# Squaring a gate on ScalarE instead of GpSimd, in a recurrence with routed experts

## The chip, the cores and the metric

The kernel runs on one core of one Trainium2 chip. A core has five engines with an in-order queue each: TensorE (PE, its weight loads shown as PEld), VectorE (DVE), ScalarE (ACT), GpSimd (POOL) and SyncE (SP, which only issues DMAs here). POOL also issues DMAs: those whose rows are addressed by a list of indices. The metric is device time in microseconds; lower is better. The kernel before takes 990.24 us, the median of three runs (990.15 to 991.3).

## The reference

A gated linear recurrence over 4 sequences of 3648 steps and 256 channels, and behind it a mixture of 16 experts (4 groups of 4) to which each of the 14592 tokens is routed:

```python
log_a = c * sig_r * np.log(np.clip(a_base, 1e-06, 1.0 - 1e-06))
a_t = np.exp(log_a)
norm = np.sqrt(np.maximum(1.0 - a_t * a_t, 1e-06))
x_gated = norm * sig_i * x
for t in range(S):
    h = a_t[:, t] * h + x_gated[:, t]
    y[:, t] = h
# for each token: best group g, best expert e in it, weights from two softmaxes
h = np.maximum(xg[mask_e] @ w1[g, e], 0.0)          # 256 -> 1024
ye = h @ w2[g, e]                                   # 1024 -> 256
out[tok_idx] = combined[:, None] * ye
```

The `a_t * a_t` in `norm` is the square that this document is about.

## The kernel before

**Chunks.** Tokens lie along the free dimension, channels on the partitions in two halves. They are worked on in 16 chunks of `SIZES` tiles of 128 tokens (4, then thirteen times 8, then 4 and 2), so a full chunk is two tiles of 128 x 1024. For each half h of a chunk: `tanh_r` (ACT, L317) and `decay` (ACT Exp, L322) make the decay `a` in place; `square` (POOL, L327) writes a*a into a new tile `v`; `norm1` (DVE, L332) subtracts and clips; `norm2` (ACT Sqrt, L337) takes the root; `gate_i` (ACT, L341) and `gated` (DVE, L345) make the gated input; `scale_s` (DVE, L349) multiplies it into `v`; `scan` (DVE, L358) runs the recurrence and leaves the outputs in `a`.

**Routing.** PE turns the chunk's outputs into rows of tokens, with the routing logits beside them (`rows1`, L367, four fp32 matmuls for two tiles of 128 tokens; the profile counts eight, as each takes two passes). ACT copies the rows out of PSUM (`rows2`, L373), DVE sums the logits (`rows3`, L381). `route1` to `route3` (DVE L390 to L442, ACT Exp L397) pick the expert, `rank` (PE, L447 and L448) numbers the tokens of each expert, `route4` (DVE, L453 to L464) makes the row index `pi`, and `scatter` (POOL, L468) sends each tile of 128 rows with one indirect DMA into the experts' lists `y_s` in DRAM. The tiles for rows get token numbers from POOL (`rows0`, L378).

**Experts.** After chunks 2 and 3 four resident experts get a first block of 128 rows each (L1024 transposes on PE, L1028 copy on ACT, L1035 and L1047 matmuls, L1040 ReLU on ACT, L1052 and L1055 the result). After chunks 4, 7 and 10 counts are taken (L596, then a chain of small DVE operations L586 to L634, L643 on PE, L650 to L671), and from them comes a list of units of 256 rows of one expert. SP gathers a unit's rows (L478) and loads its weights (L974). Twelve units run in plain fp32 (`native`: L980 transposes, L990 and L1004 matmuls), the rest as three products of split operands (L859, L928). Results are weighted (L943 on ACT, L945 on DVE) and sent to the output by an indirect DMA of POOL (L951).

**Order.** Every operation is declared with `op(engine, cost, emit, due, after, new, use, ...)`. `Plan.run` simulates the engines with these costs and due times while the program is built and emits each operation when its turn comes; each engine then runs its own queue in that order, and semaphores keep the dependences. So a cost in an `op` doesn't change what an instruction does, but where it and others stand. An ACT operation can name a table (`exp`, `sqrt`); the planner charges a switch.

Of the kernel before, what the change touches and what calls it, by code (L numbers as in the profile page):

```python
# [12 lines left out]
AF = mybir.ActivationFunctionType  # L13
ALU = mybir.AluOpType
# [30 lines left out]
class Plan:  # L45
# [14 lines left out]
    def op(self, engine, cost, emit, due, after=(), new=(), use=(), dma=0, table=None, soon=0.0, order=()):  # L60
        o = Op(engine, cost, emit, due, new, use, dma, table, soon)
        after = dict.fromkeys(a for a in after if a)
        order = dict.fromkeys(a for a in order if a and a not in after)
        o.wait = len(after) + len(order)
        for b in o.new + o.use:
            b.left += 1
        for a in after:
            a.then.append(o)
        for a in order:
            a.next.append(o)  # L70
        self.ops.append(o)
        return o
# [70 lines left out]
def rglru_moe_kernel(ctx: ExitStack, tc: tile.TileContext, x, r_gate, i_gate, a_param,  # L143
                     w_group, w_expert, w1, w2, out):
    nc = tc.nc
    V, S, G, T, DMA = nc.vector, nc.scalar, nc.gpsimd, nc.tensor, nc.sync
# [33 lines left out]
    OTURN, ONORM1, ONORM2, OGATE, OGATED, OSCAN, OH, OROWS, OY = 5, 1, 14, 12, 13, 7, 4, 16, 20  # L180
    OROUTE, ORANK, OSCAT = (34, 34, 60), 46, 50
# [43 lines left out]
    op = plan.op  # L225
# [98 lines left out]
    def square(ck, h):  # L324
        ck.t["v", h] = pools["v"].tile([P, CH * P], F32, name="v")
        a = ck.t["a", h][:, :ck.W]
        G.tensor_tensor(ck.t["v", h][:, :ck.W], a, a, op=ALU.mult)  # L327


    def norm1(ck, h):  # L330
# [135 lines left out]
    def scatter(ck, ks):  # L466
        for k in ks:
            ins = G.indirect_dma_start(out=y_s, out_offset=bass.IndirectOffsetOnAxis(ap=ck.pi[:, k:k + 1], axis=0),  # L468
                                       in_=ck.t["yo", k // 4][:, k % 4, :], in_offset=None,
                                       bounds_check=NBLK * TS - 1, oob_is_err=False)  # L470
            tc.declare_no_dep(ins.ins, group="lst", reason="rows of one list are disjoint")
            tc.declare_no_dep(ins.ins, group="got", reason="what was read lies before the rows that still come")
            tc.add_to_no_dep_group("lst", ins.ins)
            tc.add_to_no_dep_group(f"lst{ck.c}", ins.ins)
# [28 lines left out]
    def act(n):  # L503
        return 0.16 + n / 1180
# [4 lines left out]
    def add_chunk(ck, before):  # L509
        K, W, due, b = ck.K, ck.W, ck.due, ck.b  # L510
        ld = {}
        for what in "asx":
            for h in range(2):
                if ck.c:
                    at = due + LOADS[what] + 3 * h
# [5 lines left out]
        sq = {}  # L521
        for h in range(2):
            th = op("ACT", act(W), lambda h=h: tanh_r(ck, h), due + h * OTURN, [ld["a", h]], use=[b["a", h]], table="exp")
            de = op("ACT", act(W) + 0.18, lambda h=h: decay(ck, h), due + h * OTURN, [th], use=[b["a", h]], table="exp")
            sq[h] = op("POOL", 0.05 + W * 1.95 / 1024, lambda h=h: square(ck, h), due + h * OTURN, [de], [b["v", h]], [b["a", h]])
        n1 = [op("DVE", 0.3 + W / 1920, lambda h=h: norm1(ck, h), due + ONORM1 + h * 4, [sq[h]], use=[b["v", h]]) for h in range(2)]
        n2 = op("ACT", 2 * act(W), lambda: norm2(ck), due + ONORM2, n1, use=[b["v", 0], b["v", 1]], table="sqrt")
        ga = []
# [29 lines left out]
        def at(o):  # L558
            return due + (ROUTE if early else o) + urgent
# [5 lines left out]
        rk = op("PE", 0.15, lambda: rank(ck), at(ORANK), [r3, before and before.acc], [q], [b["oe"]], order=[before and before.hold])  # L565
        r4a, r4 = chain(route4(ck), [0.33, 0.28, 0.28, 0.38, 0.17], at(ORANK), [rk], [b["pi"]], [b["oe"], q])
        ck.acc = r4a
        ck.sca = [op("POOL", 2.3, lambda k=k: scatter(ck, range(k, k + 2)), at(OSCAT), [r4],
                     use=[b["pi"], yos[k // 4]], dma=2 * P * DW * 4) for k in range(0, K, 2)]


# [681 lines left out]
    due = cks[-1].due  # L1253
# [90 lines left out]
```

## Time and profile before

| | before |
|---|---|
| median of 3 runs | 990.24 us |
| profiled execution | 991.88 us |
| its span, first to last instruction | 990.2 us |
| busy PE / PEld / DVE / ACT / POOL | 870.6 / 831.4 / 665.3 / 558.4 / 349.8 us |
| squares on POOL (L327), 32 in all | 56.6 us, mean 1784 ns |
| scatters (L468), 114 in all | 141.2 us, mean 1239 ns |
| mean granted TensorE clock | 0.954 |

The page divides the span into 40 slices of 24.8 us and gives each engine's busy share in tenths:

```profile
PE   1333578999998999999999999999999999999994
DVE  4987688945976742566777777777765576566661
ACT  7866566526875632355555565555654555454541
POOL 4264657827477466211111111111112122213122
PEclk9866599989999999999999999999999999999998
```

PE is thinly used in the first five slices and nearly full from the seventh on. A group of instructions is shown as busy time, mean of one, and the idle time of its engine just before them with what ended it. Times of one execution are in microseconds from the span's start; means of one instruction are in nanoseconds.

### The profile page before, as it was taken

To read this page: it belongs to the slowest core of one execution; us is meant where nothing else is said; L and a number is where in the kernel's file an instruction comes from. 1 tells how busy PE (TensorE), PEld (TensorE's weight loads), DVE (VectorE), ACT (ScalarE), POOL (GpSimd) and SP (SyncE) were. 2 spreads that over 40 slices of the span, in tenths; PEclk is the share of its full clock that TensorE was granted. 3 is DMA by queue.
4 is the path that set the end of the run, shared out by engine and by line. 5 is a ranking of instruction groups with operands and counts; after the bars stand their busy time and mean duration, and the time that the engine had idled before them with its cause. 6 is when DMAs were issued, how large, how long until landed. Compare 5 with 4: busy or idle time off the path is not lost. (4 is left out here: it accounts for less than half of the span.)

```text
span 990.2 us, 18521 instructions
## 1 busy us (share of the span) xinstructions
PE 870.6 (88%) x6082; PEld 831.4 (84%) x6082; DVE 665.3 (67%) x1366; ACT 558.4 (56%) x847; POOL 349.8 (35%) x322
## 2 busy tenths in 40 slices
PE   1333578999998999999999999999999999999994
PEld 1332568888887898899999999999999999999984
DVE  4987688945976742566777777777765576566661
ACT  7866566526875632355555565555654555454541
POOL 4264657827477466211111111111112122213122
PEclk9866599989999999999999999999999999999998
DMA  9995465696877857656766776678665465635310
GB/s 317 415 331 199 150 219 163 199 395 245 332 250 238 310 182 232 195 168 230 229 210 222 225 221 214 219 222 278 221 208 185 137 215 158 195 116 190 110 54 21
DMA packets 72455, 213.33 MB, mean 215 GB/s; under 512 B 10503, under 2 KB 28431, under 8 KB 68240
## 3 DMA queue, kind: packets, MB, share of 16 engines
q1 hardware_dynamic: 60464, 181.82, 55.6%
q0 software_dynamic: 11872, 30.05, 8.0%
q8 instruction: 59, 0.97, 0.4%
q14 instruction: 60, 0.49, 0.2%
HBM read 181.56 MB, written 32.36 MB: 216 GB/s over the span
## 5 line engine op out<-in xcount | busy, mean ns | idle before, releaser
L951 POOL DMA_INDIRECT out_dram<-o,cl x122 | 132.5, 1086 | 477.3 <-ACT o L943 265.7
L468 POOL DMA_INDIRECT y_s<-wf,pi x114 | 141.2, 1239 | 106.9 <-issue 51.2
L367 PE MATMUL q_y<-yw,a 128*128 128x148 f32 x368 | 66.5, 329 | 65.0 <-DVE a L358 39.5
L859 PE MATMUL q_h<-x,w1h 128*128 128x384 f32 (+1 forms) x512 | 116.6, 316 | 6.0 <-DVE i L866 5.3
L367 PEld LDWEIGHTS q_y<-yw,a 128*128 128x128 f32 x368 | 60.1, 219 | 72.7 <-DVE a L358 19.5
L866 DVE SCALAR_TENSOR_TENSOR i<-q_h,a 128x384 fp32r<-128x384 f32 (+1 forms) x128 | 61.8, 496 | 86.5 <-ACT a L863 84.5
L863 ACT ACTIVATE a<-q_h 128x384 fp32r<-128x384 f32 (+1 forms) x128 | 56.5, 447 | 109.3 <-PE q_h L859 93.1
L859 PE MATMUL q_h<-xh,w1h 128*128 128x256 f32 x400 | 113.6, 284 | 0.0
L859 PE MATMUL q_h<-xh,w1l 128*128 128x256 f32 x400 | 113.2, 283 | 0.0
L859 PE MATMUL q_h<-xl,w1h 128*128 128x256 f32 x400 | 113.2, 283 | 0.0
L863 ACT ACTIVATE hh<-q_h 128x512 fp32r<-128x512 f32 x100 | 60.2, 602 | 92.7 <-PE q_h L859 82.2
L814 DVE TENSOR_TENSOR w1l<-wf,w1h 128x1024 fp32r<-128x1024 f32 x82 | 99.9, 1221 | 11.8 <-ACT w1h L812 9.8
L866 DVE SCALAR_TENSOR_TENSOR hl<-q_h,hh 128x512 fp32r<-128x512 f32 x100 | 68.8, 688 | 55.8 <-ACT hh L863 55.7
L814 DVE TENSOR_TENSOR w2l<-wf,w2h 128x1024 fp32r<-128x1024 f32 x82 | 98.2, 1218 | 0.0
L859 PEld LDWEIGHTS q_h<-x,w1h 128*128 128x128 f32 x512 | 84.9, 190 | 7.6 <-issue 5.0
L812 ACT CAST w1h<-wf 128x1024 fp32r<-128x1024 f32 x82 | 87.0, 1064 | 0.3 <-issue 0.3
L812 ACT CAST w2h<-wf 128x1024 fp32r<-128x1024 f32 x82 | 83.9, 1043 | 0.0
L859 PE MATMUL q_h<-x,w1l 128*128 128x384 f32 (+1 forms) x256 | 79.8, 312 | 0.0
L859 PEld LDWEIGHTS q_h<-xl,w1h 128*128 128x128 f32 x400 | 76.8, 192 | 0.0
L859 PEld LDWEIGHTS q_h<-xh,w1h 128*128 128x128 f32 x400 | 76.8, 192 | 0.0
L859 PEld LDWEIGHTS q_h<-xh,w1l 128*128 128x128 f32 x400 | 76.8, 192 | 0.0
L327 POOL TENSOR_TENSOR v<-a 128x1024 f32<-128x1024 f32 (+2 forms) x32 | 56.6, 1784 | 33.0 <-ACT a L322 20.4
(374 smaller groups left out, 2037.9 us busy)
## 6 DMA issues: line engine op xcount, KB each, us to landing
wf<-in_moe_w_dram SPq DMA_DIRECT2D x164, 512.0 KB, 5.0
a<-in_r_gate_dram SPq DMA_DIRECT2D x26, 512.0 KB, 9.0
i<-in_i_gate_dram SPq DMA_DIRECT2D x26, 512.0 KB, 8.9
x<-in_x_dram SPq DMA_DIRECT2D x26, 512.0 KB, 9.7
g<-y_s SPq DMA_DIRECT2D x37, 258.0 KB, 4.2
w1h<-in_moe_w_dram SPq DMA_DIRECT2D x8, 1024.0 KB, 7.8
w1l<-in_moe_w_dram SPq DMA_DIRECT2D x8, 1024.0 KB, 10.0
w2h<-in_moe_w_dram SPq DMA_DIRECT2D x8, 1024.0 KB, 8.6
```

The costliest lines, as they stand in the source:

```text
L327: G.tensor_tensor(ck.t["v", h][:, :ck.W], a, a, op=ALU.mult)
L367: T.matmul(q[:, k, h * YW:(h + 1) * YW], lhsT=ck.t["a", h][:, (2 * i + k) * P:(2 * i + k + 1) * P], rhs=yw[:, h, :], start=True, stop=True)
L468: ins = G.indirect_dma_start(out=y_s, out_offset=bass.IndirectOffsetOnAxis(ap=ck.pi[:, k:k + 1], axis=0), in_=ck.t["yo", k // 4][:, k % 4, ...
L812: S.copy(hi[m.b][:, sl], src)
L814: V.tensor_tensor(lo[m.b][:, sl], src, hi[m.b][:, sl].bitcast(F32), op=ALU.subtract)
L859: T.matmul(q, lhsT=w[m.b][:, c, fs], rhs=mv[:, c, :N], start=n == 0, stop=n == 5)
L863: S.activation(hh, q, AF.Relu)
L866: V.scalar_tensor_tensor(hl, q, 0.0, hh.bitcast(F32), op0=ALU.max, op1=ALU.subtract)
L951: ins = G.indirect_dma_start(out=out, out_offset=bass.IndirectOffsetOnAxis(ap=m.col("idx", h), axis=0), in_=m.o[h], in_offset=None, bounds ...
```

## The change

`square` becomes an ACT activation with the function Square; its `op` moves to ACT with the cost of an activation of that width. It names no table. The planner's cost of a pair of scatters goes from 2.3 to 2.6.

```diff
     def square(ck, h):
         ck.t["v", h] = pools["v"].tile([P, CH * P], F32, name="v")
         a = ck.t["a", h][:, :ck.W]
-        G.tensor_tensor(ck.t["v", h][:, :ck.W], a, a, op=ALU.mult)
+        S.activation(ck.t["v", h][:, :ck.W], a, AF.Square)
...
-            sq[h] = op("POOL", 0.05 + W * 1.95 / 1024, lambda h=h: square(ck, h), due + h * OTURN, [de], [b["v", h]], [b["a", h]])
+            sq[h] = op("ACT", act(W), lambda h=h: square(ck, h), due + h * OTURN, [de], [b["v", h]], [b["a", h]])
...
-        ck.sca = [op("POOL", 2.3, lambda k=k: scatter(ck, range(k, k + 2)), at(OSCAT), [r4],
+        ck.sca = [op("POOL", 2.6, lambda k=k: scatter(ck, range(k, k + 2)), at(OSCAT), [r4],
```

What it does to the queues, at three places. POOL, from the scatters of chunk 0 on (four of them; the next ones are of chunks 1, 2 and 3). Before:

```order
L468 DMA y_s<-wf,pi 241920x258 x4
L327 TENSOR_TENSOR v<-a 128x1024 x2
L378 IOTA wf 128x4
L468 DMA y_s<-wf,pi 241920x258 x8
L327 TENSOR_TENSOR v<-a 128x1024
L378 IOTA wf 128x4
L327 TENSOR_TENSOR v<-a 128x1024
L378 IOTA wf 128x4
L468 DMA y_s<-wf,pi 241920x258 x8
L327 TENSOR_TENSOR v<-a 128x1024
```

Now:

```order
L468 DMA y_s<-wf,pi 241920x258 x4
L378 IOTA wf 128x4
L468 DMA y_s<-wf,pi 241920x258 x8
L378 IOTA wf 128x4 x2
L468 DMA y_s<-wf,pi 241920x258 x8
```

The squares of later chunks, which stood between the scatters, are gone from this queue. ACT, ahead of the copy of the first resident block's rows (L1028), the last rows before it. Before:

```order
L373 COPY wf<-q_y 128x2x256
L341 ACTIVATE i<-i 128x1024
L373 COPY wf<-q_o 128x2x256
L317 ACTIVATE a<-a 128x1024
L322 ACTIVATE a<-a,la 128x1024
L373 COPY wf<-q_o 128x2x256
L317 ACTIVATE a<-a 128x1024
L1028 COPY xh<-q_r 128x256
L337 ACT_TABLE_LOAD
L337 ACTIVATE v<-v 128x1024 x2
```

Now:

```order
L337 ACTIVATE v<-v 128x1024 x2
L373 COPY wf<-q_o 128x2x256
L327 ACTIVATE v<-a 128x1024
L341 ACT_TABLE_LOAD
L341 ACTIVATE i<-i 128x1024
L373 COPY wf<-q_y 128x2x256
L397 ACTIVATE e__850<-d__841 128x160
L341 ACTIVATE i<-i 128x1024
L317 ACTIVATE a<-a 128x1024 x2
L322 ACTIVATE a<-a,la 128x1024
L1028 COPY xh<-q_r 128x256 x2
```

Ahead of that copy stand now 12 squares of 1024 and two of 512, and two square roots, two table loads, a row copy (L373) and an Exp (L397) more than before; the numbers of L317, L322 and L341 are the same. PE, around the first unit (L990). Before:

```order
L367 MATMUL q_y<-yw,a 128x148 x4
L980 MATMUL q_r<-yw,g 128x128 x4
L1047 MATMUL q_o<-w2l_180,hh 128x256 x4
L367 MATMUL q_y<-yw,a 128x148 x4
L1047 MATMUL q_o<-w2l_180,hh 128x256 x4
L990 MATMUL q_h<-xh,w1h_1547 128x256 x4
```

Now:

```order
L980 MATMUL q_r<-yw,g 128x128 x4
L1047 MATMUL q_o<-w1l_178,hh 128x256 x8
L1035 MATMUL q_h<-xh,w2h_179 128x128 x8
L367 MATMUL q_y<-yw,a 128x148 x4
L1035 MATMUL q_h<-xh,w2h_179 128x128 x8
L1047 MATMUL q_o<-w2l_180,hh 128x256 x4
L367 MATMUL q_y<-yw,a 128x148 x4
L1047 MATMUL q_o<-w2l_180,hh 128x256 x4
L367 MATMUL q_y<-yw,a 128x148 x4
L990 MATMUL q_h<-xh,w1h_1464 128x256 x4
```

The transposes of the first unit's rows (L980) stand ahead of more of the resident blocks' work, and 116 row matmuls (L367) stand ahead of the first L990, where there were 108. From row 216 of PE's 6735 on, and from row 295 of ACT's 1676, the queues hold the same rows in the same order as before, apart from buffer numbers.

## The prediction

> **What bounds the kernel now.** I read the busy time by stages first, and put the borders where TensorE's own rows change: 119.30, where the first resident block's matmuls (L1035) begin; 207.95, where the first early unit (L990) begins; 424.30, where the split units (L859) begin; 966.90, the last piece of the chain. In each row the span is followed by busy time of PE, PEld, DVE, ACT and POOL.
>
> ```profile
> core 0: us, PE busy (x) PEld busy (x) DVE busy (x) ACT busy (x) POOL busy (x), PEclk, DMA share, GB/s
> 0.00:119.30 119.30, 40.90 (x159) 35.37 (x159) 85.95 (x178) 82.86 (x94) 59.92 (x63) 0.73 0.79 290
> 119.30:207.95 88.65, 76.47 (x484) 69.80 (x484) 74.23 (x150) 53.99 (x71) 57.93 (x43) 0.91 0.63 208
> 207.95:424.30 216.35, 207.08 (x1095) 182.76 (x1093) 129.09 (x437) 115.67 (x173) 122.53 (x117) 0.99 0.72 255
> 424.30:966.90 542.60, 535.87 (x4267) 533.34 (x4265) 372.01 (x594) 302.67 (x503) 103.58 (x94) 1.00 0.61 193
> 966.90:990.20 23.30, 10.30 (x84) 10.13 (x84) 4.05 (x10) 3.19 (x8) 5.83 (x6) 0.80 0.07 21
> ```
>
> From 207.95 on PE is the bound (207.08 of 216.35, then 535.87 of 542.60). What PE computes is the same in both kernels, so the end moves only as far as PE's idle time moves: 78.4 us of it lie before 119.30, 12.2 in the second stage, 9.3 in the third. Before 119.30 PE waits for the chunks, and a chunk goes through ACT, POOL, DVE, ACT, DVE. The second view is what DVE and POOL do there, in order of time (start, duration, engine, line, in brackets the idle time before and who ended it):
>
> ```profile
> 80.15 2.46 DVE L332 TENSOR_SCALAR v<-v 128x1024 f32<-128x1024 f32 x1 [5.17 <-POOL v L327]
> 95.21 0.37 DVE L428 TENSOR_TENSOR oe<-d__603 128x128 f32<-128x128 f32 x1
> 102.88 0.15 DVE L454 TENSOR_TENSOR cacc<-cacc,cn 128x16 bf16<-128x16 bf16 x1
> 108.27 4.39 DVE L332 TENSOR_SCALAR v<-v 128x1024 f32<-128x1024 f32 x1 [5.23 <-POOL v L327]
> 115.84 0.17 DVE L464 CAST pi<-pos 128x8 int32<-128x8 f32 x1 [0.16 <-DVE lgs L381]
> 115.92 0.69 DVE L332 TENSOR_SCALAR v<-v 128x1024 f32<-128x1024 f32 x1
> 132.22 2.37 DVE L332 TENSOR_SCALAR v<-v 128x1024 f32<-128x1024 f32 x1 [2.90 <-POOL v L327]
> 134.92 2.83 DVE L428 TENSOR_TENSOR oe<-d__863 128x128 f32<-128x128 f32 x1
> 151.17 2.40 DVE L332 TENSOR_SCALAR v<-v 128x1024 f32<-128x1024 f32 x1
> ```
>
> ```profile
> 94.16 1.31 POOL L468 DMA_INDIRECT y_s<-wf,pi  x1 [11.51 <-DVE pi L464]
> 105.33 0.98 POOL L468 DMA_INDIRECT y_s<-wf,pi  x1 [0.30 <-DMA y_s<-wf,pi]
> 106.32 1.91 POOL L327 TENSOR_TENSOR v<-a 128x1024 f32<-128x1024 f32 x1
> 108.26 1.91 POOL L327 TENSOR_TENSOR v<-a 128x1024 f32<-128x1024 f32 x1
> 110.19 1.90 POOL L327 TENSOR_TENSOR v<-a 128x1024 f32<-128x1024 f32 x1
> ```
>
> Two losses show. First, a square stands on POOL behind eight scatters (94.16 to 106.31), so DVE, which has nothing it may do before it, stands from 103.03 to 108.27. Second, the L332 that then starts needs 4.39 us, not the 0.69 of 115.92: it ends at 112.66, just after the two squares at 108.26 and 110.19 (112.09). DVE's L332 does not get through while POOL squares. Chunk 3's scatter indices (L464, 115.84) are behind both.
>
> **The change, part by part.** The groups up to 208 us give the size of both losses (busy us, mean ns, idle before):
>
> ```profile
> DVE v L332 <- POOL v L327: 17.5, 5, 5.2
> L332 DVE TENSOR_SCALAR v<-v 128x1024 f32<-128x1024 f32 x18 | 24.3, 1351 | 17.5 <-POOL v L327 17.5
> L327 POOL TENSOR_TENSOR v<-a 128x1024 f32<-128x1024 f32 x18 | 36.2, 2021 | 31.6 <-ACT a L322 19.1 <-DVE a L358 12.4
> L468 POOL DMA_INDIRECT y_s<-wf,pi x44 | 63.0, 1431 | 44.6 <-issue 21.7 <-DVE pi L464 15.4 <-DVE t L690 4.7
> ```
>
> Removed: 17.5 us of waiting on DVE, and 18 x (1.351 - 0.69) = 11.9 us of L332 in excess, with single rows such as L428 above (2.83 at 134.92, 0.37 at 95.21) on top: about 30 us of DVE's first 208. The 36.2 us that POOL is freed of are no gain in themselves; the scatters keep their 1431 ns.
>
> Added on ACT: 32 squares. The trace has no Square on ACT; the nearest row is a Tanh over the same tile with constant scale (L341, below, 1052 ns). A square is the same pass with a cheaper function, so I take 1.05 us. From below, 0.95: neighbours on ACT overlap by some 0.1 (two Exps of 1.235 take 2.36, the row at 97.70 below). From above, 1.235, what that Exp (L322) with its two operand columns takes. The spread, 0.2 us x 14 squares, is under 3 us at the place that counts.
>
> Term 1, the start of the first block (119.30). It waits for the copy of its rows on ACT, at 117.20. What ACT had done by then (the window's row), its longest waits up to 119.3, and its groups up to 208 us and one pair of rows, for the durations:
>
> ```profile
> 0.00:117.20 117.20, 38.80 (x150) 33.29 (x151) 85.34 (x173) 80.79 (x91) 58.13 (x62) 0.74 0.80 294
> ACT wf L373 <- DVE lgs L381: 11.8, 4, 8.7
> ACT v L337 <- DVE v L332: 7.9, 4, 3.8
> ACT wf L373 <- PE q_y L367: 6.3, 3, 3.5
> ACT a L317 <- DMA a<-in_r_gate_dram: 5.0, 2, 3.9
> L341 ACT ACTIVATE i<-i 128x1024 f32<-128x1024 f32 x20 | 20.8, 1052 | 4.0 <-DMA i<-in_i_gate_dram 3.9
> L322 ACT ACTIVATE a<-a,la 128x1024 f32<-128x1024 f32 x18 | 21.9, 1235 | 0.2
> 97.70 2.36 ACT L322 ACTIVATE a<-a,la 128x1024 f32<-128x1024 f32 x2
> L337 ACT ACT_TABLE_LOAD x9 | 11.5, 1283 | 0.1
> L373 ACT COPY wf<-q_y 128x512 f32<-128x512 f32 x16 | 9.3, 579 | 12.4 <-PE q_y L367 12.4
> ```
>
> ACT was busy 80.8 us and idle 36.4. In the new order more stands ahead of that copy: 12 squares of 1024 and two of 512 (12 x 1.05 + 2 x 0.6 = 13.8), two square roots (2.1), two table loads (2 x 1.28 = 2.6), a copy and an Exp (0.58 + 0.3): 19.4 us, some 17.9 when the overlap of 0.1 between neighbours is taken off. So ACT's work there becomes 98.7 us, and its idle time decides. Of the 36.4, 7.9 end with L332 itself and 11.8 with the L381 rows that stand behind L332 on DVE (the largest, 8.7, ends just after the 4.39 us row). Without these 16.7 are left. As ACT comes later to the rows of PE that it copies, part of its waits for PE (6.3) goes too; the waits for the inputs (5.0) stay. I take 11.3: copy at 110.0, first matmul half a microsecond behind, as the last row group of that chunk now stands ahead of the transposes: 110.5, **-8.8 us**. Bounds: with 5.0 idle 104, -15; with all 16.7 idle 116, -3.
>
> That only stands if the rows are there to be copied: chunk 2's scatters end at 106.31 now and are gathered after that. They begin at 94.16, when chunk 2's indices are there, and ahead of that three of DVE's five waits for POOL lie, 17.5 - 5.23 - 2.90 = 9.4 us. Without these the last scatter ends at 97, and with 4 us to land and to be gathered (an estimate: 117.2 - 106.31 is 10.9 with a row group on PE in between) the rows are there at 101, 9 us ahead of ACT. That is the cover that keeps ACT, not POOL, on the path.
>
> Term 2, PE's 12.2 us idle from 119.30 to 207.95. These are the gaps:
>
> ```profile
> 135.05 1.27 PE L367 MATMUL q_y<-yw,a 128*128 128x148 f32 x8 [2.06 <-DVE lgs L381]
> 140.64 3.24 PE L1047 MATMUL q_o<-w2l,hh 128*128 128x256 f32 x8 [3.88 <-ACT wf L373]
> 153.85 5.41 PE L1047 MATMUL q_o<-w1l,hh 128*128 128x256 f32 x16 [2.71 <-DVE lgs L381]
> 200.06 1.11 PE L980 MATMUL q_r<-yw,g 128*128 128x128 f32 x4 [3.00 <-DMA g<-y_s]
> 207.95 1.89 PE L990 MATMUL q_h<-xh,w1h 128*128 128x256 f32 x8
> 209.68 1.17 PE L367 MATMUL q_y<-yw,a 128*128 128x148 f32 x8
> ```
>
> The first three (8.65) follow the stalled rows at 132.22, 134.92 and 151.17 and go. ACT, busy 53.99 of 88.65 now, gets four squares more in the stretch (4.2), and the ReLUs and row copies for which PE waits stand behind them in its queue: I give 2.6 back. **-6.0 us**, bounds -10 (only small change left) and +4 (nothing gained, each square late once).
>
> Term 3: 116 row matmuls (29 groups) now stand ahead of the first unit, 108 (27) before. Two groups at 1.17, less overlap: 2 us that move from behind to ahead, nothing in the sum. The first unit starts at 207.95 - 8.8 - 6.0 + 2 = 195.2.
>
> Term 4, the third stage: 14 squares remain, ten of 1024, two of 512, two of 256, 12.5 us on ACT, which rises from 115.67 to 128 of 216. They are hidden by PE's 207 us; without that cover they would cost up to 12.5. DVE is rid of further waits that PE does not feel. 0, from -4 to +6.
>
> Term 5: from 424.30 on the queues hold the same rows in the same order. 0. The longer scatter time in the planner (2.6) costs nothing on the chip; it acts through the order, which is counted above.
>
> Sum: 991.88 (the profiled execution: 990.2 span, 1.7 around it) - 8.8 - 6.0 = 977.1. The median of the runs lies 1.64 below the profiled execution, so **975.5 us**.
>
> **The rivals.** *ACT takes over (slower).* If ACT's idle time ahead of the first copy is not the squares' doing but the price of its turns with PE and DVE, the 17.9 us come on top in full: copy at 135.1, first matmul at 135.6, +16.3; with term 2 still gained, 991.88 + 16.3 - 6.0 - 1.64 = 1000.5. It decides from 26 us of idle ahead of the copy on: 98.7 + 26.1 + 0.5 = 125.3, where a first block 6.0 us late uses up term 2. For it speaks that ACT is the busiest engine beside DVE there (82.86 of 119.30) and that 1.91 us on an idle engine become 1.05 on a busy one; against it, that 19.7 of the 36.4 us end with L332 or rows right behind it.
>
> *Given back later (about the same).* The chunks 8 to 15 are not sped up, since PE's queue paces them; their rank and count steps, which stand between the units in PE's queue, come late, and PE's 9.3 us of third-stage idle grow to 24: 990. At half of that, 983. For it: four gaps there already; against it: DVE is busy only 129 of 216.
>
> *DVE's whole loss comes back (faster).* All of the 30 us of DVE count: first block at 104 (-15), term 2 at -10, term 4 at -4: 961. Against it stands ACT's 98.7 us of work ahead of the copy.
>
> *It does not do what it says.* Were Square no member of the tables that Exp and Sqrt use, each chunk's squares would need a switch and one back, 2 x 1.283 us; for the seven chunks ahead of the first copy that is 18 us on top of the slower rival, 1018. Both programs hold 33 table loads, none of them at a square; one square even stands between a square root and the load for the next Tanh. So I give it no chance. [...]
>
> **How the numbers follow.** Forecast, 965 to 985 with 975.5 as its value: 0.60. More (below 965): 0.10. Given back to between 985 and 992: 0.12. ACT takes over or other losses, above 992: 0.18. Two in ten are left out with 961 to 994. A difference under 0.2% (2 us) cannot be told from none here: faster (under 988.3) 0.60 + 0.10 + 0.06 = 0.76, the same 0.06, slower 0.18.
>
> **What would show it.** In the new profile: no DVE L332 over 0.75 us that overlaps a POOL operation other than a scatter, and no wait of L332 for POOL; the new L327 rows on ACT near 1.05 us; the first L1035 near 110 (not over 117), the first L990 near 195, the first L859 near 410; ACT idle near 11 us before the first L1028, and busy about 0.9 of that stretch. The forecast is wrong if ACT's idle before that copy stays over 20 us, if PE's idle between the first L1035 and the first L990 is not under 10 us, or if the stretch from the first L990 to the first L859 has over 15 us of idle PE.

## The result and the profile after

The changed kernel takes 960.21 us (median of 4 runs, 959.16 to 962.99), the kernel before 990.77 beside it (990.15 to 992.24): a ratio of 0.969, with an interval of 0.967 to 0.972. That is 30.6 us less, twice the 15 us of the forecast. It lies 4.8 us below the range of the forecast (965 to 985) and 0.8 us below the 961 to 994 that were to hold in eight cases of ten. The profiled execution takes 959.16 us, with a span of 957.4.

The chips on which the later runs were made differ: the kernel before takes 990 to 993 us on some of them and 1008 to 1016 on others. So every experiment is read by its ratio to the kernel before on its own chip. On one of the second kind the change was timed again: 0.969 (0.967 to 0.971). Two runs of kernels below, of 1005.4 and 985.2 us, were over 1.5% longer than the fastest of their kernel, which marks a slower state, and are left out of its time and ratio.

The stages of the changed kernel, with the borders at the same rows as before (first L1035, first L990, first L859, last piece of the chain); the last row ends at the first copy of a resident block's rows:

```profile
core 0: us, PE busy (x) PEld busy (x) DVE busy (x) ACT busy (x) POOL busy (x), PEclk, DMA share, GB/s
0.00:106.95 106.95, 37.86 (x158) 32.67 (x159) 79.58 (x191) 98.00 (x112) 44.68 (x54) 0.69 0.86 323
106.95:182.98 76.03, 72.37 (x500) 67.56 (x500) 64.14 (x147) 55.63 (x73) 40.33 (x33) 0.98 0.76 257
182.98:392.60 209.62, 205.24 (x1080) 181.38 (x1078) 119.69 (x426) 123.53 (x184) 105.25 (x105) 0.98 0.73 258
392.60:934.10 541.50, 534.98 (x4261) 532.64 (x4259) 371.71 (x594) 302.58 (x502) 104.07 (x94) 1.00 0.62 193
934.10:957.40 23.30, 11.19 (x92) 10.81 (x90) 4.43 (x11) 3.24 (x8) 5.88 (x6) 0.82 0.07 22
0.00:104.90 104.90, 37.38 (x156) 32.20 (x156) 79.12 (x188) 97.67 (x112) 43.02 (x52) 0.70 0.86 325
```

Against the rows of before:

| stage | length before, after | PE idle before, after | forecast for the step |
|---|---|---|---|
| to the first L1035 | 119.30, 106.95 | 78.4, 69.1 | -8.8 |
| to the first L990 | 88.65, 76.03 | 12.2, 3.7 | -6.0, and 2 us of rows more |
| to the first L859 | 216.35, 209.62 | 9.3, 4.4 | 0, and 2 us of rows less |
| the rest | 565.90, 564.80 | 19.7, 18.6 | 0 |

Over the span PE's idle time falls by 23.8 us (119.6 to 95.8) and its busy time by 9.0 (870.6 to 861.6): together the 32.8 us of the two spans.

The groups that the change touches, up to 183 us, and the waits of DVE for ACT there (in groups: busy us, mean ns, idle before; in the wait: total, times, longest):

```profile
L332 DVE TENSOR_SCALAR v<-v 128x1024 f32<-128x1024 f32 x18 | 12.6, 711 | 3.7 <-ACT v L327 3.7
L327 ACT ACTIVATE v<-a 128x1024 f32<-128x1024 f32 x18 | 19.0, 1056 | 2.0 <-DVE mA L671 1.9
L468 POOL DMA_INDIRECT y_s<-wf,pi x44 | 65.9, 1498 | 60.1 <-DVE w__372 L421 41.3 <-issue 9.4 <-ACT xh L1028 2.5
DVE v L332 <- ACT v L327: 6.6, 5, 2.8
```

A Square takes 1056 ns on ACT, as assumed. L332 is back at 711 ns (1351 before), and of the 17.5 us for which DVE waited for POOL's square 6.6 us are left as a wait for ACT's. POOL now waits for work (60.1 us idle ahead of the scatters, 44.6 before).

How the first block starts, in order of time on DVE, POOL, SP, ACT and PE (start, duration, instruction, idle time before):

```profile
81.65 0.17 DVE L464 CAST pi<-pos 128x8 int32<-128x8 f32 x1
82.65 2.51 POOL L468 DMA_INDIRECT y_s<-wf,pi  x1 [2.30 <-DVE a L358]
94.77 0.98 POOL L468 DMA_INDIRECT y_s<-wf,pi  x1 [0.30 <-issue]
101.72 1.51 SPq L478 DMA_DIRECT2D hl<-y_s  x2
101.64 1.23 ACT L322 ACTIVATE a<-a,la 128x1024 f32<-128x1024 f32 x1
104.14 0.69 PE L1024 MATMUL q_r<-yw,hl 128*128 128x128 f32 x2 [8.05 <-DMA hl<-y_s]
104.86 0.37 ACT L1028 COPY xh<-q_r 128x256 f32<-128x256 f32 x1 [1.99 <-PE q_r L1024]
106.95 4.89 PE L1035 MATMUL q_h<-xh,w1h 128*128 128x128 f32 x32
```

Chunk 2's indices are there at 81.82, its eight scatters lie between 82.65 and 95.75 (106.31 before), the gather follows at 101.72, and PE has waited 8.05 us for it when the transposes start at 104.14. ACT, free at 102.87, waits another 1.99 us for PE. It was idle 104.90 - 97.67 = 7.2 us ahead of that copy.

### The profile page after: what moved, and what is told of

Its sections match the earlier page's. It is cut to its first block, busy times and chain, and to the rows that moved or that the text cites. A ratio compares the mean times of both kernels' runs of the same rounds, so it can differ in the third digit from the quotient of the medians.

```text
span 957.4 us, 18539 instructions
## 1 busy us (share of the span) xinstructions
PE 861.6 (90%) x6082; PEld 825.1 (86%) x6082; DVE 639.6 (67%) x1366; ACT 583.0 (61%) x879; POOL 300.2 (31%) x290
## 5 line engine op out<-in xcount | busy, mean ns | idle before, releaser
L951 POOL DMA_INDIRECT out_dram<-o,cl x122 | 135.7, 1112 | 477.0 <-ACT o L943 275.3
L859 PE MATMUL q_h<-x,w1h 128*128 128x384 f32 (+1 forms) x512 | 116.7, 316 | 5.9 <-DVE i L866 5.2
L859 PE MATMUL q_h<-xh,w1h 128*128 128x256 f32 x400 | 113.7, 284 | 0.0
L859 PE MATMUL q_h<-xh,w1l 128*128 128x256 f32 x400 | 113.3, 283 | 0.0
L859 PE MATMUL q_h<-xl,w1h 128*128 128x256 f32 x400 | 113.2, 283 | 0.0
L367 PE MATMUL q_y<-yw,a 128*128 128x148 f32 x368 | 63.2, 318 | 46.0 <-DVE a L358 30.6
L367 PEld LDWEIGHTS q_y<-yw,a 128*128 128x128 f32 x368 | 57.6, 211 | 52.7 <-DVE a L358 16.9
L859 PEld LDWEIGHTS q_h<-x,w1h 128*128 128x128 f32 x512 | 84.9, 190 | 7.5 <-issue 5.0
L859 PE MATMUL q_h<-x,w1l 128*128 128x384 f32 (+1 forms) x256 | 79.9, 312 | 0.0
L859 PEld LDWEIGHTS q_h<-xl,w1h 128*128 128x128 f32 x400 | 76.8, 192 | 0.0
L859 PEld LDWEIGHTS q_h<-xh,w1h 128*128 128x128 f32 x400 | 76.8, 192 | 0.0
L859 PEld LDWEIGHTS q_h<-xh,w1l 128*128 128x128 f32 x400 | 76.8, 192 | 0.0
L358 DVE TENSOR_TENSOR_SCAN a<-a,v 128x1024 f32<-128x1024 f32 (+8 forms) x38 | 67.4, 1792 | 0.0
```

What stands on the lines that cost most here:

```text
L358: V.tensor_tensor_scan(a[:, sl], a[:, sl], v[:, sl], init, ALU.mult, ALU.add)
L367: T.matmul(q[:, k, h * YW:(h + 1) * YW], lhsT=ck.t["a", h][:, (2 * i + k) * P:(2 * i + k + 1) * P], rhs=yw[:, h, :], start=True, stop=True)
L859: T.matmul(q, lhsT=w[m.b][:, c, fs], rhs=mv[:, c, :N], start=n == 0, stop=n == 5)
L951: ins = G.indirect_dma_start(out=out, out_offset=bass.IndirectOffsetOnAxis(ap=m.col("idx", h), axis=0), in_=m.o[h], in_offset=None, bounds ...
```

## The experiments

Each kernel is the changed one with the edit shown, unless said otherwise. What was expected is quoted as written before the runs; the first four are in microseconds of a chip on which the kernel before takes 990, and theirs took 1014.8, so they are compared by their distance from the kernel before. Ratios of two chips are to be compared with care: one kernel that was timed on two chips of the slower kind came to 0.954 and 0.961 (below).

### The two halves of the change

The square on ACT with the scatters' planning cost left at 2.3:

```diff
-        ck.sca = [op("POOL", 2.6, lambda k=k: scatter(ck, range(k, k + 2)), at(OSCAT), [r4],
+        ck.sca = [op("POOL", 2.3, lambda k=k: scatter(ck, range(k, k + 2)), at(OSCAT), [r4],
```

> The square on ScalarE, the planner's cost of a pair of scatters left at 2.3. Theory A (the gain comes from freeing VectorE of the squares on GpSimd: the wait for them behind scatters, and the stall beside them): at least three quarters of the 30.6 us stay, 958 to 968. Rival B (the re-planned order with the longer scatter time is what helps): under half stays, 975 to 990.

The other half alone, the kernel before with 2.6:

```diff
-        ck.sca = [op("POOL", 2.3, lambda k=k: scatter(ck, range(k, k + 2)), at(OSCAT), [r4],
+        ck.sca = [op("POOL", 2.6, lambda k=k: scatter(ck, range(k, k + 2)), at(OSCAT), [r4],
```

> The square stays on GpSimd, only the planner's cost of a pair of scatters is 2.6. Theory A: VectorE's waits and stalls stay, 985 to 995, L332 still above 1.2 us on average up to the first unit. Rival B: a gain of 15 us or more, below 976.

Since both also change the order, two more kernels hold the order still. The changed kernel's order row for row, with each square on POOL at its place:

```diff
-        S.activation(ck.t["v", h][:, :ck.W], a, AF.Square)
+        G.tensor_tensor(ck.t["v", h][:, :ck.W], a, a, op=ALU.mult)
```

> The order of the changed kernel on every engine, kept row for row, but the squares run on GpSimd at the place where they are emitted. Theory A: the order alone brings nothing; squares stand between scatters again and VectorE waits, 985 to 1005. Rival B: the order carries the gain, below 972.

And the order of the kernel before on all other engines, with each square on ACT:

```diff
-        G.tensor_tensor(ck.t["v", h][:, :ck.W], a, a, op=ALU.mult)
+        S.activation(ck.t["v", h][:, :ck.W], a, AF.Square)
```

> The order of the kernel before on every engine, but the squares run on ScalarE at the place where they are emitted, behind the decay. Theory A: most of the gain is there without any new order, 962 to 973; L332 near 0.7 us and no wait for GpSimd. Rival B: under half of it, above 976. In both the pauses of TensorE between the first block and the first unit are under 8 us by A and over 10 by B.

| kernel | time | ratio to before, interval |
|---|---|---|
| square on ACT, cost 2.3 | 985.16 | 0.972 (0.969 to 0.975) |
| cost 2.6 alone | 1007.69 | 0.993 (0.990 to 0.996) |
| order of the change, square on POOL | 1003.22 | 0.990 (0.987 to 0.993) |
| order of before, square on ACT | 986.42 | 0.974 (0.970 to 0.978) |

On this chip the move to ACT is worth 2.6% with the order of before held and 2.8% with an order planned for it, the planner's number alone 0.7% and the change's order alone 1.0%; the 3.1% of the whole change were measured on other chips. So the engine makes most of the gain. Order alone brought 7 and 12 us, more than theory A allowed and far less than rival B asked for. With 2.6 alone L332 takes 1056 ns (above 1.2 us was expected) and waits 9.1 us for POOL in place of 17.5. DVE's L332 up to the first L990, first with the change's order and POOL's squares, then with the order of before and ACT's:

```profile
L332 DVE TENSOR_SCALAR v<-v 128x1024 f32<-128x1024 f32 x18 | 15.5, 875 | 17.0 <-POOL v L327 17.0
```

```profile
L332 DVE TENSOR_SCALAR v<-v 128x1024 f32<-128x1024 f32 x18 | 12.2, 680 | 1.4 <-ACT v L327 1.4
```

The new order alone takes most of the stretch from L332 (875 ns) but none of the waiting (17.0 us), and gains 1.0%. The engine alone takes both. One sign of theory A failed there: with the order of before and ACT's squares PE is idle 10.7 us between the first block and the first unit, where under 8 was expected; its first block starts at 104.2, ahead of the change's.

### The squares of the later chunks

Chunks 0 to 7 as in the change, chunks 8 to 15 on POOL, with POOL's cost in the `op`:

```diff
-        S.activation(ck.t["v", h][:, :ck.W], a, AF.Square)
+        if ck.c < 8:
+            S.activation(ck.t["v", h][:, :ck.W], a, AF.Square)
+        else:
+            G.tensor_tensor(ck.t["v", h][:, :ck.W], a, a, op=ALU.mult)
```

> The squares of chunks 0 to 7 on ScalarE, those of chunks 8 to 15 on GpSimd as before, with GpSimd's cost in the order. If all of the gain is made by the first eight chunks (TensorE is the bound from 208 us on): ratio 0.969 to 0.971, as for the change whole. If the later chunks count as the third stage's 4.9 us less of idle TensorE say: 4 to 7 us lost, ratio 0.973 to 0.977, with TensorE idle 8 to 10 us between the first L990 and the first L859.

969.91 us, ratio 0.977 (0.972 to 0.982). The second and third stage of it, DVE's L332 over both (L335 in this file) and its longest wait of PE in the third:

```profile
107.10:190.00 82.90, 75.08 (x509) 69.45 (x508) 70.16 (x152) 57.06 (x74) 50.55 (x39) 0.97 0.73 250
190.00:405.10 215.10, 205.73 (x1069) 180.96 (x1069) 128.05 (x420) 107.69 (x165) 124.23 (x115) 0.98 0.70 247
L335 DVE TENSOR_SCALAR v<-v 128x1024 f32<-128x1024 f32 x15 | 13.3, 890 | 8.2 <-POOL v L330 8.2
PE q_y L450 <- DVE lgs L384: 6.4, 1, 6.4
```

The first block starts at 107.1 as in the change, the first split unit at 405.1 and not 392.6. By the medians some 7 of the 30 us come from chunks 8 to 15, by the interval 3 to 12: with their squares on POOL, DVE waits for POOL again (8.2 us), and PE, which was to be the bound there, waits for DVE's logits (6.4 us, once).

### ScalarE as the next bound

Each square issued twice on ACT:

```diff
         S.activation(ck.t["v", h][:, :ck.W], a, AF.Square)
+        S.activation(ck.t["v", h][:, :ck.W], a, AF.Square)
```

> The kernel after the change with each square issued twice on ScalarE (same output). 14 squares more ahead of the first copy, 14 x 1.05 = 14.7 us of ScalarE work; it was idle 7.2 us before that copy. If ScalarE is the next bound there: first L1035 at 114 to 122 (7.5 to 15 us later), ratio to the kernel before 0.977 to 0.985. If the gather of the rows stays the bound: first L1035 under 110, ratio 0.969 to 0.973.

973.85 us, ratio 0.981 (0.978 to 0.983). Its first stage:

```profile
0.00:115.20 115.20, 40.63 (x158) 34.67 (x158) 80.16 (x192) 111.74 (x127) 44.86 (x52) 0.68 0.80 298
```

13.7 us more of ACT's work (111.74 busy against 98.00) move the first block by 8.2, and the end by 11 (1.1%). So ACT, idle 7.2 us there, is the next bound, some 5 us behind the one that holds.

### GpSimd's own time

What of POOL's relief counts: its time, DVE's rows beside it, or the hand-over? Four kernels leave the squares on ACT and give POOL work on a tile of its own, for which nothing waits. Eight small multiplications per full square:

```diff
+    spare = const.tile([P, P], F32, name="spare")
+    V.memset(spare, 1.0)
...
         S.activation(ck.t["v", h][:, :ck.W], a, AF.Square)
+        for z in range(0, ck.W, P):
+            z = min(P, ck.W - z)
+            G.tensor_tensor(spare[:, :z], spare[:, :z], spare[:, :z], op=ALU.mult)
```

> The kernel after the change, with work on GpSimd that nothing waits for: at each square GpSimd also multiplies a 128x128 tile of its own eight times (once per 128 columns of the square), which VectorE neither reads nor writes. The square itself stays on ScalarE. If VectorE loses time by GpSimd's running beside it: L332 rows over 0.75 us again where they overlap these multiplications, a part of VectorE's 11.9 us of excess back, first L1035 some 4 to 9 us later, ratio 0.973 to 0.982. If only the wait for the square in GpSimd's queue cost time: L332 at 0.71 us throughout, ratio within 0.969 to 0.972.

1020.56 us, ratio 1.029 (1.027 to 1.031): slower than the kernel before, beyond either expectation. The small tiles cost 624 ns each, 5 us per square. So the dose was taken down. Four products of 128x256:

```diff
+    spare = const.tile([P, 2, P], BF16, name="spare")
+    four = ident.unsqueeze(1).broadcast_to([P, 2, P])
...
+        for z in range(0, ck.K, 2):
+            n = min(2, ck.K - z)
+            G.tensor_tensor(spare[:, :n], four[:, :n], four[:, :n], op=ALU.mult)
```

> The kernel after the change, with work on GpSimd that nothing waits for: at each square (which stays on ScalarE) GpSimd multiplies a 128x256 tile of its own four times, the same number of elements as the square it was freed of, on tiles that VectorE does not touch. Some 2 to 2.5 us of GpSimd per square are expected, half of what the eight 128x128 multiplications took. If GpSimd's time ahead of the scatters is what counts: first L1035 some 5 to 10 us later than the changed kernel's, ratio to the kernel before 0.985 to 1.0, L332 at 0.71 to 0.77. If VectorE is held up by the mere presence of such work on GpSimd: L332, the scan and the other rows with two inputs grow by 10% or more in the mean and account for most of the loss. If neither counts: 0.969 to 0.973.

985.5 us, ratio 0.993 (0.990 to 0.996). POOL's spare products, its scatters and DVE's L337 (L332 in the kernel before) up to the first L990, and PE's wait:

```profile
L332 POOL TENSOR_TENSOR spare<-yw 128x256 bf16<-128x256 f32 x76 | 67.6, 889 | 4.9
L337 DVE TENSOR_SCALAR v<-v 128x1024 f32<-128x1024 f32 x18 | 14.1, 789 | 3.1 <-ACT v L329 3.0
PE q_r L1029 <- DMA hl<-y_s: 21.5, 3, 19.0
```

3.6 us per square take away three quarters of the gain, and the way shown is through the scatters: PE waits up to 19.0 us for the first gather, and the first block starts at 122.3, 15 us later than in the change (5 to 10 were expected). Then half of it, two products per full square, 1.5 us:

```diff
-        for z in range(0, ck.K, 2):
-            n = min(2, ck.K - z)
+        for z in range(0, ck.K, 4):
+            n = 2
```

> The kernel after the change, with two multiplications of 128x256 on GpSimd at each whole square (half of what the run with four had, some 1.8 us, near the 1.9 us of the square that it was freed of), which read and write tiles that nothing else waits for. By the run with four of them (0.993, VectorE's busy time 23 us up), half: ratio to the kernel before 0.978 to 0.987, VectorE's busy time 8 to 15 us over the changed kernel's 639.6. If only the first few us per square can be hidden and the loss is steep beyond them: 0.969 to 0.975.

And the same time on POOL without reading, eight memsets:

```diff
+    spare = const.tile([P, P], F32, name="spare")
...
+        for z in range(ck.K):
+            G.memset(spare, 1.0)
```

> The kernel after the change, with one 128x128 memset on GpSimd per 128 columns of each square (eight at most, 0.2 us each by the one of this size in the trace, so 1.6 us per square): GpSimd's time is about that of the run with two multiplications, but it only writes. If the queue sets the loss (scatters behind GpSimd's work): the same ratio as that run, 0.978 to 0.987. If VectorE's rows beside GpSimd's reads set it: 0.969 to 0.974, VectorE's busy time within 4 us of 639.6.

979.29 us, ratio 0.964 (0.962 to 0.965), with the products; 984.95 us, 0.970 (0.968 to 0.972), with the memsets. To read these the changed kernel was run again with no edit, on another chip of the slower kind:

> The changed kernel itself, once more, since the chips of the runs differ (the kernel before takes 990 us on some and 1015 on others) and the change itself was only timed on one of the first kind. If the chip only scales the stages: ratio to the kernel before 0.966 to 0.972 on either kind, and the two multiplications (0.964) and the memsets (0.970) cost nothing that can be measured. If the later start that those two show (first L1035 at 112 instead of 107, as traced) reaches the end: 0.958 to 0.965 on a chip on which the kernel before takes 1015.

976.7 us, ratio 0.969 (0.967 to 0.971). By these ratios neither run shows a loss, but the two chips are not alike. The kernel with squares on DVE and 3.3 (below) ran on both, with 969.52 us and 0.954 on the chip of the products and memsets, 969.68 us and 0.961 on this one: its time is the same, that of the kernel before is not (1015.8 and 1008.0). By time the products lose 2.6 us against the change and the memsets some 8. So a loss of up to 8 of the 30 us is not excluded. The first stage of the two (first the products, then the memsets), POOL's extra work and L332's counterpart:

```profile
0.00:111.90 111.90, 38.34 (x158) 33.27 (x159) 87.09 (x191) 98.29 (x112) 63.08 (x79) 0.68 0.82 306
L332 POOL TENSOR_TENSOR spare<-yw 128x256 bf16<-128x256 f32 x38 | 29.0, 764 | 1.9
L337 DVE TENSOR_SCALAR v<-v 128x1024 f32<-128x1024 f32 x18 | 13.2, 743 | 2.3 <-ACT v L329 2.2
```

```profile
0.00:112.20 112.20, 38.88 (x159) 34.02 (x160) 79.60 (x192) 98.03 (x112) 60.10 (x156) 0.68 0.81 304
L330 POOL MEMSET spare<- 128x128 f32 x152 | 32.8, 216 | 7.9
L335 DVE TENSOR_SCALAR v<-v 128x1024 f32<-128x1024 f32 x18 | 12.7, 717 | 4.6 <-ACT v L328 4.6
```

In the first stage POOL is as busy as in the kernel before (63.08 and 60.10; 59.92 before), and the first block starts 5 to 6 us later than in the change, at 112. With the products DVE's rows are stretched (87.09 us busy in that stage, 79.60 with the memsets), with the memsets not; the start is the same. So the start hangs on POOL's queue and not on DVE's stretched rows. Nor do these cost anything at the end that shows: on the same chip the run with them is the faster one. What the later start costs at the end may be more on the first chip, since in the third stage PE is idle 18.1 us in the changed kernel on the slower kind and 4.4 us on the first.

What the kernel before has beside the same load on POOL is that L332 waits for a square that stands in that queue. The kernel with the change's order and POOL's squares is nearest to these two: the same order, 36.1 us of squares on POOL up to the first unit against 29.0 and 32.8 us of spare work. Its first block starts at 126.5, theirs at 112, the change's at 106 to 107; its ratio is 0.990, theirs are 0.964 and 0.970. So 5 to 6 of these 20 us go with POOL's time and some 14 with what is left, and the runs point to the hand-over as the larger part of the gain. They don't prove its size by itself: the spare work is a little less than the squares, the ratios are of two chips, and no kernel here kept the hand-over and freed POOL of the time.

### TensorE's pauses

In the trace of the change PE's rows are slow after a pause:

```profile
299.02 3.78 PE L1004 MATMUL q_o<-w1l,hh 128*128 128x256 f32 x8 [4.34 <-ACT o L943]
302.59 2.55 PE L990 MATMUL q_h<-xh,w1h 128*128 128x256 f32 x8
```

Each such group takes 1.89 us elsewhere. A sweep of pauses, made by repeating the ReLU that PE waits for, more often from unit to unit:

```diff
-        S.activation(m.hh[j], q, AF.Relu)
+        for _ in range(1 + max(0, m.u - 1)):
+            S.activation(m.hh[j], q, AF.Relu)
```

> The kernel after the change, in which early unit number u (L990 and L1004) issues its ReLU on ScalarE 1 + max(0, u - 1) times, so that TensorE's pauses inside the third stage grow from unit to unit; the output is the same, since a ReLU of a ReLU changes nothing. Theory A (after a pause of more than about 2.7 us TensorE's rows run at half speed for 2 to 4 us): groups of eight 128x256 rows take 1.89 us behind pauses up to 2.4 us, and 2.7 to 3.8 us behind pauses over 3 us, and what is lost again per long pause stays near 2 to 3 us however long the pause is. Rival (the slow rows come from something else at that time, a transfer or ScalarE): slow groups do not follow the length of the pause. The total is not of interest; some 40 to 120 us longer.

1029.61 us. Rows of PE in it, in order of time:

```profile
308.66 2.34 PE L367 MATMUL q_y<-yw,a 128*128 128x148 f32 x8 [3.03 <-DVE lgs L381]
367.20 1.99 PE L1005 MATMUL q_o<-w1l,hh 128*128 128x256 f32 x8 [2.47 <-DVE o L945]
383.31 3.60 PE L1005 MATMUL q_o<-w1l,hh 128*128 128x256 f32 x8 [2.65 <-ACT hh L997]
421.25 3.40 PE L1005 MATMUL q_o<-w1l,hh 128*128 128x256 f32 x8 [2.59 <-ACT hh L997]
429.28 1.99 PE L1005 MATMUL q_o<-w1l,hh 128*128 128x256 f32 x8 [2.77 <-ACT hh L997]
443.08 1.99 PE L1005 MATMUL q_o<-w2l,hh 128*128 128x256 f32 x8 [3.50 <-DVE t L615]
```

The length of the pause alone doesn't decide. After 2.59, 2.65 and 3.03 us the next group runs at about half speed; after 2.47, 2.77 and even 3.50 at full. In this sweep pauses under 1.8 us cost nothing. The expected bound of 2.7 us does not hold; that slow groups stand only behind pauses does.

What decides is in the clock that the trace has beside the rows. All twenty changes of the granted clock from 45.26 to 424.14 us lie whole multiples of 3.41 us apart, wherever the pauses stand; so do the 19 of the kernel before (42.24 to 980.91 us). Five stretches of that grid (PE's busy time stands behind the length, the granted clock is the third figure from the end):

```profile
417.31:420.73 3.42, 1.35 (x6) 0.84 (x5) 0.00 (x0) 3.23 (x7) 0.00 (x0) 1.00 0.94 327
420.73:424.14 3.41, 2.89 (x7) 2.35 (x8) 1.98 (x2) 3.38 (x5) 0.00 (x0) 0.50 0.32 130
437.79:441.21 3.42, 1.79 (x9) 1.24 (x7) 0.00 (x0) 3.26 (x6) 0.00 (x0) 1.00 0.00 0
441.21:444.62 3.41, 1.54 (x7) 1.38 (x8) 2.01 (x12) 3.32 (x8) 1.53 (x2) 1.00 0.11 5
444.62:448.03 3.41, 3.27 (x17) 1.88 (x15) 2.70 (x22) 3.22 (x7) 0.43 (x1) 1.00 0.82 225
```

The pause of 2.59 us leaves PE idle for 2.07 us of one stretch, and the next one has half the clock. The pause of 3.50 us is split between two, which are idle 1.63 and 1.87 us, and the clock stays. In the third stage of this run a stretch at full clock is followed by half the clock when PE was idle in it for 1.88 us or more, never below that; in the kernel before, from 36 us on, up to 1.84 us cost nothing and 1.93 us and more did. A few stretches of other runs depart from this bound, between 1.7 and 2.8 us. So a pause counts by how it falls on the grid, and a group is slow as long as it lies in a stretch at half the clock. A stretch need not be idle as a whole: 2.07 us of 3.42 were enough at 417.31.

### What is left to gain

The squares on DVE instead:

```diff
-        S.activation(ck.t["v", h][:, :ck.W], a, AF.Square)
+        V.tensor_tensor(ck.t["v", h][:, :ck.W], a, a, op=ALU.mult)
...
-            sq[h] = op("ACT", act(W), lambda h=h: square(ck, h), due + h * OTURN, [de], [b["v", h]], [b["a", h]])
+            sq[h] = op("DVE", dve(W), lambda h=h: square(ck, h), due + h * OTURN, [de], [b["v", h]], [b["a", h]])
```

> The kernel after the change, with the 32 squares on VectorE in place of ScalarE (planned with VectorE's cost). Theory A (the gain is that VectorE and the scatters are rid of GpSimd's squares, wherever the squares then stand): the squares cost VectorE between 0.7 and 1.3 us each, 14 of them ahead of the first copy of a resident block, 10 to 18 us on an engine that was idle 27 of its first 107 us; so most of the gain stays, ratio to the kernel before 0.972 to 0.985, first L1035 at 110 to 118. Theory B (the gain comes from ScalarE doing the square just behind its Exp, in its own queue): the ratio goes to 0.99 or above, first L1035 at 119 or later.

954.96 us, ratio 0.962 (0.960 to 0.964): better than the change, and than either expectation. The first stage and the square:

```profile
0.00:105.80 105.80, 35.96 (x158) 31.24 (x159) 85.61 (x189) 85.46 (x96) 40.35 (x52) 0.72 0.89 323
L327 DVE TENSOR_TENSOR v<-a 128x1024 f32<-128x1024 f32 x18 | 21.7, 1212 | 2.7 <-ACT a L322 2.7
```

A square costs DVE 1212 ns and ACT 1056, but it stands ahead of L332 in the same queue, and ACT is 12.5 us less busy. Which engine has the square matters less than that it isn't POOL.

A longer time for scatters in the planner, 3.3 for two (with ACT's squares):

```diff
-        ck.sca = [op("POOL", 2.6, lambda k=k: scatter(ck, range(k, k + 2)), at(OSCAT), [r4],
+        ck.sca = [op("POOL", 3.3, lambda k=k: scatter(ck, range(k, k + 2)), at(OSCAT), [r4],
```

> The kernel after the change with the scatters' time in the planner at 3.3 in place of 2.6. Its one effect is on the order. The change of 2.3 to 2.6 was worth 0.3 to 1.0% in the runs above. If the planner still takes the scatters as too short (their median from issue to the next is 1.3 to 1.6 us each, two in a step): ratio to the kernel before 0.960 to 0.967. If 2.6 is already right: 0.967 to 0.975.

955.69 us, ratio 0.963 (0.961 to 0.966). Its first and third stage:

```profile
0.00:113.10 113.10, 42.51 (x175) 36.68 (x176) 85.91 (x201) 105.18 (x120) 48.19 (x57) 0.74 0.86 319
184.60:387.90 203.30, 203.30 (x1085) 180.43 (x1084) 118.29 (x416) 122.00 (x182) 106.04 (x105) 1.00 0.73 255
```

The first block starts later (113.10), with more of PE's work ahead of it, and PE has no idle time at all in the third stage.

The clip folded into DVE's square, and L332 left out:

```diff
-        V.tensor_tensor(ck.t["v", h][:, :ck.W], a, a, op=ALU.mult)
+        V.scalar_tensor_tensor(ck.t["v", h][:, :ck.W], a, 1.0 - 2.0 ** -21, a, op0=ALU.min, op1=ALU.mult)
...
-            S.activation(v, v, AF.Sqrt, scale=-0.25)
+            S.activation(v, v, AF.Sqrt, scale=-0.25, bias=quarter)
```

> Squares on VectorE as one operation with the limit, min(a, 1 - 2^-21) * a, and the subtraction from 1 as the bias of the square root on ScalarE, so that L332 (0.71 us, 32 of them) is left out; the floor under the root is 5e-7 and not 1e-6. Against the run with plain squares on VectorE (0.962): 14 x 0.72 = 10 us less of VectorE ahead of the first copy and one hand-over less. If VectorE or the chain square, L332, root sets the time: ratio to the kernel before 0.948 to 0.957, first L1035 at 95 to 102. If ScalarE and the gather set it: 0.959 to 0.964, first L1035 at 103 to 107.

953.76 us, ratio 0.961 (0.959 to 0.963): 10 us less of DVE up to the first unit (140.1 busy, 150.4 with the plain squares) bring nothing that can be told from the plain squares. DVE no longer sets the time.

Squares on DVE and 3.3 together, and the same with the clip folded in (the edits are those above):

> Squares on VectorE (0.962 alone) and the scatters' time in the planner at 3.3 (0.963 alone, against 0.969 of the change). If the two take from different losses: 0.954 to 0.958. If both use up the same reserve (TensorE's 4 to 8 us idle behind the first block): 0.960 to 0.964.

> As the run before it, with the limit folded into VectorE's square and L332 left out (floor under the root 5e-7 instead of 1e-6; 0.961 alone). If what is left is the first stage, in which VectorE is 10 us lighter: 0.950 to 0.956. If the inputs and the scatters set the first stage: the same as the run before it, within 0.003.

969.52 us, ratio 0.954 (0.952 to 0.956), and 974.42 us, 0.957 (0.954 to 0.960). The first of them once more, beside the unedited change on the same chip:

> Squares on VectorE and 3.3 for the scatters in the planner, beside the change on the same chip. If this is the better version on every chip: 0.008 to 0.016 below the change's ratio. If its 0.954 came from the chip of that call: the same as the change within 0.004.

969.68 us, ratio 0.961 (0.959 to 0.964), where the change has 976.7 us and 0.969. So it beats the kernel before on both of its chips, by 3.9 to 4.6%, and the change by 0.7% on the one chip where both ran, a little less than the 0.8 to 1.6% expected. Whether the two gains add stays open: 0.954 says yes, while 0.961 is about what each gave alone (0.962 and 0.963).

## Why the prediction was wrong

The mechanism and its place were right: L332 waited for POOL's squares, the waits are gone, the square costs 1056 ns on ACT (1.05 assumed), no table load is added (33 in both), ACT's work ahead of the first copy is 97.67 us (98.7 worked out), and the stages from 424 us on are unchanged. The forecast was half as large as the gain, and these steps failed. In the spans it gave 14.8 us where 32.8 came. Of the 18 us that it lacked, 9.0 are busy time of PE, which it put at nothing, and 9.0 are idle time of PE, 4.9 of these in the third stage, which it put at nothing too.

**"The end moves only as far as PE's idle time moves."** PE's idle time gave 23.8 us, and its busy time another 9.0. In the kernel before PE's rows are slow behind pauses too: the 16 rows of L1047 at 153.85 took 5.41 us behind 2.71 us of waiting, the eight at 140.64 took 3.24 behind 3.88; those at full clock take 1.89 for eight. The granted clock in the second stage rose from 0.91 to 0.98. I quoted these rows and read only the brackets in them. A pause removed is worth its length and, where it had cost the clock, what the slow rows take beyond that: 1.4 us (3.24 - 1.89) and 1.6 us (5.41 - 2 x 1.89) for these two.

**Term 1, -8.8; measured -12.35** (9.3 of PE's idle and 3.0 of its busy time). The idle time of ACT ahead of the first copy was put at 11.3 and is 7.2. The waits for PE's rows, of which a part was to stay, are gone (6.3 us behind q_y before), and of the 5.0 us for the inputs, which were to stay whole, 2.1 are left. The cover named for it did not hold: I had the rows gathered by 101, 9 us ahead of ACT, with an estimate of 4 us from the end of the scatters. They ended at 95.75 (97 worked out), but PE got its rows at 104.14, 8.4 us later. So the gather came last: 1.99 of the 7.2 us are ACT's wait for it. ACT is close behind, as the doubled squares show.

**Term 2, -6.0; measured -8.5 of idle time,** within its bounds. Gaps of 3.7 us are left, these two, one of 0.33 us for ACT (L373, at 135.31) and one of 1.06 us for DVE (L671, at 151.85):

```profile
113.75 2.00 PE L1047 MATMUL q_o<-w1l,hh 128*128 128x256 f32 x8 [1.69 <-ACT hh L1040]
117.55 1.99 PE L1047 MATMUL q_o<-w1l,hh 128*128 128x256 f32 x8 [0.58 <-ACT hh L1040]
```

The waits for ACT's ReLUs and copies come to 2.6 us, as much as was given back; that is luck, since the longest stands behind a gate that waited 2.50 us for its input (L341, 112.16), not behind a square. What the term left out is the gap of 3.00 us at 200.06, a wait for the first unit's gather, which is gone as well.

**Term 3** holds: the rows moved ahead. The first L990 comes at 183.0, not 195.2, by the sizes of terms 1 and 2 and by PE's faster rows.

**Term 4, 0; measured -6.7, of which 2 are rows moved ahead.** "Hidden by PE's 207 us" was wrong twice. PE's idle time in that stage fell by 4.9 us, to 4.4 (one pause of 4.34 is left); and with the squares of chunks 8 to 15 back on POOL the time is 0.7% worse. That PE is 96% busy in a stage does not hide a chain on which its few pauses hang.

**The removed losses of DVE** were right in size (of 17.5 us of waiting 6.6 came back as a wait for ACT; 11.9 us of stretch up to 208) but not equal in worth: in the run with two products stretched rows of DVE cost nothing that shows at the end, and the runs point to the wait for the square.

**The rivals.** "DVE's whole loss comes back", at 0.10, gave 961; that is the time that came, though not by its parts: the first block at 106.95 and not 104, and the rest from PE's faster rows, so the hit is luck. "ACT takes over" did not come true: ACT's idle time was 7.2 us, far from the 26 at which it was to decide. "Given back later" is the opposite of what happened in the third stage.

## What to carry to other kernels

An engine whose queue holds long DMA issues is a bad place for a small step of a chain: the runs here point less to its 1.9 us of work than to the eight scatters it stood behind (12.15 us, from 94.16 to 106.31), and a move to either of two busier engines paid. Price a pause of TensorE at its length plus the slow rows behind it (1.4 and 1.6 us at the two above), which stand in the trace of before, and look at the granted clock in stretches of 3.41 us: here about 1.9 us of idle time in one of them halved the clock of the next. And look whether the bound engine of a stage still has pauses: the few per cent of idle time in the third stage here (9.3 of 216.35 us) are where a shorter chain paid, with 4.9 us.

## What the runs showed of the hardware

VectorE lost far more beside GpSimd's products, which read and write, than beside its memsets, which only write. Over the whole run DVE is busy 639.6 us in the change, 640.2 with the memsets, 654.9 with two products per square and 662.6 with four, though it waits for none of that work. Up to the first unit two products per square take 29.0 us of POOL and the memsets 32.8. Whether a memset slows L332, its mean doesn't decide (717 ns in the run with memsets, 711 in the change): of its 26 full rows in the memset run only six overlap a memset, of which three take 0.77 to 0.80 us and three 0.68 to 0.71, as most of the others do. In the kernel before ten of the 26 overlap a square on POOL, and nine of these take 2.19 to 4.39 us, all others 0.66 to 0.69.

Small products on GpSimd were dear here: a 128x128 one took 624 ns, a 128x256 one 764 to 889 (the larger number where more of them stood together), while a square of 128x1024 took 2021 in the mean in the kernel before.

From the first split unit to the end the kernel takes 564.8 to 566.2 us in every run but the sweep of pauses (569.0), on every chip. What differs between chips lies ahead of that: on the chip on which the kernel before takes 1008 us the change's first two stages last 105.8 and 77.1 us, as on the first chip, but its third 226.8 and not 209.6, with 18.1 us of idle PE in place of 4.4. The runs don't show why.
